# Two seams of a three-stage kernel re-ordered: one pair's weight sums on VectorE, other banks and an earlier first gate tile at the first seam

## The chip, the cores and the metric

The kernel runs on one core of a Trainium2 chip. The metric is the device time of one execution in microseconds (us), as the median of several runs; less is better. The engines are named as in the profile: PE is TensorE, DVE is VectorE, ACT is ScalarE, POOL is GpSimd, SP is SyncE, which issues most DMAs (its DMA queue is SPq).

## The reference

Attention with a decay by blocks, then two MLPs one after the other, all in float32:

```python
# q, k, v: (2, 8, 768, 64); lam: (8,)
for b in range(nb):                                  # blocks of 64 tokens
    intra = einsum('bhic,bhjc->bhij', qb, kb) * Dmask[None]
    intra = einsum('bhij,bhjd->bhid', intra, vb)
    inter = einsum('bhid,bhde->bhie', qb * lam_pow[None], kv_state)
    out[:, :, sl] = intra + inter
    kv_state = lam_block * kv_state + einsum('bhsd,bhse->bhde', kb_dec, vb)
x = out.transpose(0, 2, 1, 3).reshape(1536, 512)
h = x @ w_in                                         # 512 x 2048
x = (h * np.cos(h)) @ w_out                          # 2048 x 512
h = x @ w2_in
y = (h * (1.0 / (1.0 + np.exp(-h)))) @ w2_out        # 1536 x 512
```

## The kernel before

**Precision.** Every float32 operand of the MLPs is split in a high part (an ACT CAST, line 121) and a low part (value minus high part, line 122, on POOL unless an engine is named). A product is then three matmuls: high by high, low by high, high by low.

**Stages.** Attention runs over six chunks of 128 tokens per sequence. Then come four GEMMs: in 0 (to about 190 us of the trace), out 0 (to about 335), in 1 (to about 455), out 1. The stretch where attention and GEMM in 0 overlap (about 50 to 92 us) is called the passage. The first seam is the step from GEMM in 0 to out 0, the second from out 0 to in 1, the third from in 1 to out 1.

**GEMM in.** The 2048 hidden features are taken in eight pairs j of 256. For two thirds of the tokens (quad A) pair j is computed by seven products of sums of blocks in place of eight, A*j*.1 to A*j*.7 (`product(Q, i)`, 6 matmuls each, line 429). For the last third (quad B) it is plain: B*j*, 24 matmuls, line 445. Products 5, 6 and 7 need sums or differences of the weights of a pair:

- `rebias_w` (ACT, L106) and `convert_w` (DVE, L115 writes `sb`, L116 writes `w`) turn a loaded weight piece (`raw`) into floats.
- `sum_w` makes the four sums `S` of a pair (four 128x256 operations, L134).
- `split_plain` and `split_sums` make the split weights `win` from `w` and from `S`.

`copy_u`, `c22`, `c21` and `copy_ab` put the quad's results together. Each of the two halves of a quad, and each B, then passes the gate: `act_n` (ACT, L482), `act_s` (DVE, L491), `act_sin` (ACT, L498), `act_g` (DVE, L504), whose result goes to DRAM (`gd<-s`).

**GEMM out.** Features are taken in 16 pieces f of 128, tokens in thirds b = 0, 1, 2. `gemm_out(L, b, f, ms)` does four output blocks m, three matmuls each (line 703); b = 2 comes last, alone. In the text (b, f, lo) is m = 0, 1 and (b, f, hi) is m = 2, 3. The gate's results are loaded back (`gf`, by `load_half`, `load_halves`, `load_g`) and split into `gh` and `gl` (`prepare_half` for one third of one piece, `prepare` for two). Output weights pass `rebias_w`, `convert_w` and `split_out` (`wout`).

**PSUM.** There are three pairs of banks (`cab` 0, 1, 2, by `two_banks`) and two single ones (`d`, by `one_bank`). In GEMM in 0, A*j* uses pair j modulo 2 and every B uses pair 2. In GEMM out 0, third 0 uses pairs 0 and 1; third 1 uses pair 2 and the two single banks.

**Order.** `manual_schedule` means that each engine and queue executes its instructions in the order in which the code issues them. So the order of the calls in the body, and the dictionary `tasks`, which hangs weight work onto places of the loops, decide what stands behind what. Loads of weights go through one list (`load_next`). Tiles live in pools of few slots (`t4` four, `t2` five, `w` four): an instruction that writes a tile waits for the last reader of the slot's tile before.

Of the kernel before, what the change touches and what calls it, by code (L numbers as in the profile page):

```python
# [18 lines left out]
TB = 512  # L19
# [21 lines left out]
def tile_decay_attention__two_mlps(  # L41
# [12 lines left out]
    nc = tc.nc  # L54
# [5 lines left out]
    FT = DFF // P  # L60
# [82 lines left out]
        a = 0 if L == 0 else HB  # L143
        split(hi[:, TB + a:2 * TB], lo[:, TB + a:2 * TB], w1[:, a:])

    def split_sums(L, j):
        t = win[L, j]
        s = sums.pop((L, j))
        for i in range(2):
            u = slice(4 + 2 * i, 6 + 2 * i)  # L150
            split(t[:, 0, u], t[:, 1, u], s[:, 2 * i:2 * i + 2])

    def split_out(L, f):
        t = wring[f // 8].tile([P, 2, TB], F32R, name="wout")
# [3 lines left out]
    def pair_tasks(L, j, engine=nc.gpsimd):  # L158
        f = 2 * j
        return [  # L160
            lambda: rebias_w(L, f, 0),
            lambda: (rebias_w(L, f + 1, 0), convert_w(L, f, 0), load_next()),
            lambda: (convert_w(L, f + 1, 0), load_next()),
            lambda: sum_w(L, j, engine),
            lambda: split_plain(L, j),
            lambda: split_sums(L, j),
        ]

    def out_tasks(L, f):
# [246 lines left out]
    def product(Q, i):  # L416

        wu, xu, bank, start = PRODUCTS[i]
        if i == 1:
            n = Q.j if Q.L == 0 else quads.index(Q)  # L420
            Q.cab = two_banks(n % 2 if Q.L == 0 else (n + 2) % 3)
            Q.d = one_bank(n % 2)
            Q.banks = {"a": Q.cab[:, 0, 0:Q.n], "b": Q.cab[:, 1, 0:Q.n], "d": Q.d[:, 0:Q.n]}
            if Q.L == 0 and n < 2:
                nc.tensor.matmul(Q.cab[:, 1, :], zeros[:, 0:P], zeros, start=True, stop=True)
        w, (xh, xl) = win[Q.L, Q.j], xt[Q.L, Q.part]
        for m, (part, x) in enumerate(((0, xh), (1, xh), (0, xl))):
            for kt in range(2):
                nc.tensor.matmul(  # L429
                    Q.banks[bank],  # L430
                    w[:, part, wu, kt * P:(kt + 1) * P],
                    x[:, xu, kt, :],
                    start=start and m == 0 and kt == 0,
                    stop=m == 2 and kt == 1,
                    skip_group_check=True,
                )

    def plain(Q, i):

        if i == 0:  # L440
            Q.cab = two_banks(2)
        w, (xh, xl) = win[Q.L, Q.j], xt[Q.L, Q.part]
        for m, (part, x) in enumerate(((0, xh), (1, xh), (0, xl))):
            for kt in range(KT):
                nc.tensor.matmul(  # L445
                    Q.cab[:, i],
                    w[:, part, 2 * i + kt // 2, kt % 2 * P:(kt % 2 + 1) * P],
                    x[:, kt, :],
                    start=m == 0 and kt == 0,
                    stop=m == 2 and kt == KT - 1,  # L450
                )
# [58 lines left out]
    def gemm_in_0(tasks):  # L510
# [51 lines left out]
        act_g(old, 1)  # L562
        act_n(Bq, 0)
        act_s(Bq, 0)
        load_halves(0)
        load_g(0, 0, 2)
        load_g(0, 0, 3)
        gemm_out(0, 0, 0, (0, 1))
        task(FP, 1)
        act_sin(Bq, 0)  # L570
        act_g(Bq, 0)
        gemm_out(0, 0, 1, (0, 1))
        prepare_half(0, 1, 0)
        prepare_half(0, 1, 1)
        prepare(0, 0, 2)

    def gemm_in_1(tasks):
# [65 lines left out]
            for i in range(2):  # L643
                gf[L, 2, f + i] = t[:, i]

    def load_half(L, f):
        t = tpool.tile([P, TB], F32, tag="t2", name="gf", bufs=5)
        nc.sync.dma_start(out=t, in_=gd[L][f, :, 0:TB])
        gf[L, "half", 0, f] = t

    def load_halves(L):
        t = tpool.tile([P, 2, TB], F32, tag="t4", name="gf", bufs=4)
# [28 lines left out]
    def y_tiles(L, b):  # L681
        if (L, b) not in ys:
            if b == 1:
                t = two_banks(2)
                ys[L, b] = [t, None, t[:, 0], t[:, 1]] + [one_bank(i) for i in range(2)]
            else:
                t = [two_banks(i) for i in range(2)]
                ys[L, b] = t + [t[m // 2][:, m % 2] for m in range(4)]
        return ys[L, b]

# [90 lines left out]

    def gemm_outs(L, tasks):

        items = [x for f in range(FT + 2) for x in ((0, f), (1, f - 2)) if 0 <= x[1] < FT]
        items += [(2, f) for f in range(FT)]
        for b, f in items:
            if L == 1 and b == 2 and f >= FT - 2:
                break
            if b == 0:
                load_g(L, 0, f + 4)  # L790
                prepare(L, 0, f + 2)
# [9 lines left out]
            gemm_out(L, b, f, (2, 3) if b == 0 and f < 2 else range(4))  # L801
            for x in tasks.get((b, f), []):
                x()
        if L == 1:
# [5 lines left out]
    with tc.manual_schedule():  # L810
# [84 lines left out]
        A, c = quads_a, SC - 1  # L895
        att_scores(c, 0, ps_s, "s")
        split_sums(0, 0)
        product(A[0], 1)
        copy_ab(A[0])
        att_l(c - 1)  # L900
        att_scores(c, 1, ps_s, "s")
        rebias_w(0, 3, 0)
        convert_w(0, 3, 0)
        load_next()
        sum_w(0, 1, nc.gpsimd)
        product(A[0], 2)
# [26 lines left out]
        rebias_w(0, 4, 0)  # L933
        rebias_w(0, 5, 0)

        def place(tasks, at_n, fns):
            for i, x in enumerate(fns):
# [5 lines left out]
        for L in range(2):  # L943
            tasks = {}
            if L == 0:
                for j in range(2, FP):
                    f = 2 * j
                    if j > 2:
                        put((j - 2, 2), *(lambda f=f + i: rebias_w(0, f, 0) for i in range(2)))
                    for i in range(2):  # L950
                        put((j - 1, 0), lambda f=f + i: convert_w(0, f, 0), load_next)
                    put((j - 1, 0), lambda j=j: sum_w(0, j, nc.gpsimd))
                    put((j - 1, 1), lambda j=j: split_plain(0, j))
                    put((j - 1, 2), lambda j=j: split_sums(0, j))
                for n, f in ((6, 0), (6, 1), (7, 2), (7, 3)):
                    put((n, 2), lambda f=f: rebias_w(0, f, 1))
                    put((n + 1, 0), lambda f=f: convert_w(0, f, 1), load_next)
                    put((n + 1, 1), lambda f=f: split_out(0, f))
                put((FP - 1, 0), lambda: load_half(0, 0), lambda: load_half(0, 1))
                gemm_in_0(tasks)  # L960
            else:
                for j in range(2, FP):
                    at_n = min(4 * j - 8, 18)
                    for n, x in zip((0, 1, 2, 2, 3, 4), pair_tasks(L, j)):
                        put(at_n + n, x)
                for f, n in enumerate((20, 22, 24, 25)):
# [55 lines left out]
```

## Time and profile before

| | |
|---|---|
| median of 3 runs | 595.28 us (594.83, 597.52, 595.28) |
| the profiled execution | 592.26 us, its span 590.5 us |
| TensorE clock granted, mean of the span | 0.990 |
| PE busy | 564.3 us, 96% of the span |
| POOL busy | 350.9 us, 59% |
| DVE busy | 347.8 us, 59% |
| ACT busy | 295.7 us, 50% |

Times in the trace count from the span's start. The profiled execution is 1.8 us longer than its span and 3.0 us shorter than the median. A clock of 1.00 is TensorE's full 2.4 GHz, 0.50 is its other level of 1.2 GHz.

### The profile page before, as it was taken

What the parts mean: (1) busy time and instruction counts of PE and PEld (TensorE: products, weight loads), DVE (VectorE), ACT (ScalarE), POOL (GpSimd) and SP (SyncE); (2) the same over time, 40 slices, a digit from 0 to 9 for tenths busy, and PEclk for the clock granted to TensorE, in tenths of its full rate; (3) what the DMA queues carried; (4) which work ended last, traced back from release to release, by engine and by line L of the source; (5) the groups of instructions that cost most, each with busy time, mean ns of one, the idle gap of its engine ahead of it and who ended that gap; (6) DMA issues with size and microseconds to landing.
All of it is one profiled execution on the core that took longest, in us unless ns stands there. A gap on an engine that the chain in (4) does not pass through costs nothing.

```text
span 590.5 us, 8374 instructions
## 1 busy us (share of the span) xinstructions
PE 564.3 (96%) x3168; PEld 464.3 (79%) x3168; DVE 347.8 (59%) x355; ACT 295.7 (50%) x440; POOL 350.9 (59%) x261
## 2 busy tenths in 40 slices
PE   7999799999997699999999999999799999999997
PEld 4888587777776488888888788888689888888885
DVE  6689257776677599900499246667666799302001
ACT  4566267777776655310571365666656665201220
POOL 2688635555553699940489338555754699911541
PEclk9999999999998889999999999999999999999999
DMA  9999145445445886740044026455466896205501
GB/s 177 210 233 240 37 141 178 158 153 178 160 166 195 282 329 238 246 144 0 1 143 144 1 72 236 162 182 190 157 241 226 299 319 198 71 1 196 182 15 72
DMA packets 79640, 97.02 MB, mean 164 GB/s; under 512 B 40688, under 2 KB 57072, under 8 KB 79600
## 3 DMA queue, kind: packets, MB, share of 16 engines
q1 hardware_dynamic: 77360, 95.96, 50.8%
q10 hardware_dynamic: 2240, 0.53, 0.5%
q8 instruction: 25, 0.41, 0.3%
q14 instruction: 15, 0.12, 0.1%
HBM read 68.16 MB, written 28.31 MB: 163 GB/s over the span
## 4 chain that ended last, share of the span: by engine, by line
PE 72%; DVE 9%; POOL 6%; issue 4%; DMA 3%; ACT 3%; SPq 1%; ACTq 0%; DVEq 0%; POOLq 0%
PE cab L703 30%; PE cab L429 20%; PE d L429 8%; PE d L703 7%; PE cab L445 6%; DVE xal L122 2%; DVE S L134 2%; POOL win L122 2%; DVE sb L115 1%; DMA q<-in_q_dram 1%; DVE w L116 1%; ACT s L486 1%; DMA v<-in_v_dram 1%; POOL S L134 1%; DMA gf<-gd 1%
## 5 line engine op out<-in xcount | busy, mean ns | idle before, releaser
L122 POOL TENSOR_TENSOR gl<-gf,gh 128x512 fp32r<-128x512 f32 (+1 forms) x68 | 128.6, 1898 | 97.0 <-ACT gh L121 73.3
L703 PE MATMUL cab<-gh,wout 128*128 128x512 f32 x320 | 100.3, 395 | 2.4 <-ACT gh L121 2.4
L703 PE MATMUL cab<-wout,gh 128*128 128x512 f32 x320 | 98.6, 390 | 0.0
L121 ACT CAST gh<-gf 128x512 fp32r<-128x512 f32 (+1 forms) x68 | 53.5, 795 | 85.9 <-DMA out_dram<-o 29.3
L116 DVE SCALAR_TENSOR_TENSOR w<-w,sb 128x512 uint32<-128x512 uint32 x64 | 90.1, 1408 | 9.5 <-ACT w L106 3.2
L429 PE MATMUL cab<-xah,win 128*128 128x512 f32 x320 | 86.9, 394 | 0.2 <-ACT cab L459 0.2
L703 PEld LDWEIGHTS cab<-gh,wout 128*128 128x128 f32 x320 | 61.2, 191 | 15.6 <-ACT gh L121 2.8
L134 POOL TENSOR_TENSOR S<-w 128x256 f32<-128x256 f32 x28 | 30.6, 1091 | 69.6 <-DVE w L116 69.6
L703 PEld LDWEIGHTS cab<-wout,gh 128*128 128x128 f32 x320 | 59.9, 188 | 12.1
L429 PEld LDWEIGHTS cab<-xah,win 128*128 128x128 f32 x320 | 58.9, 188 | 12.8 <-ACT cab L459 0.6
L703 PE MATMUL cab<-gl,wout 128*128 128x512 f32 x160 | 63.7, 398 | 3.9 <-POOL gl L122 3.9
L122 POOL TENSOR_TENSOR wout<-w,wout 128x512 fp32r<-128x512 f32 x32 | 51.4, 1612 | 21.1 <-ACT wout L121 21.1
L115 DVE TENSOR_SCALAR sb<-raw 128x512 uint32<-128x512 uint32 x64 | 61.0, 954 | 3.0 <-DMA raw<-in_moe_w_out_dram 2.0
L703 PE MATMUL cab<-wout,gl 128*128 128x512 f32 x160 | 62.3, 389 | 0.0
L122 POOL TENSOR_TENSOR win<-S,win 128x512 fp32r<-128x512 f32 x32 | 46.5, 1474 | 7.6 <-ACT win L121 7.6
L429 PE MATMUL cab<-xal,win 128*128 128x512 f32 x160 | 49.5, 391 | 0.0
L466 ACT COPY u<-cab 128x512 f32<-128x512 f32 (+1 forms) x48 | 24.6, 513 | 46.9 <-PE cab L429 46.9
L778 DVE COPY o<-cab 128x512 f32<-128x512 f32 x10 | 6.7, 689 | 67.7 <-PE cab L703 65.3
L106 ACT ACTIVATE w<-raw 128x512 f32<-128x512 f32 x64 | 41.9, 671 | 7.3 <-POOL wout L122 3.4
L429 PE MATMUL d<-xah,win 128*128 128x512 f32 x128 | 36.9, 400 | 5.7 <-POOL win L122 2.7
L703 PEld LDWEIGHTS cab<-gl,wout 128*128 128x128 f32 x160 | 30.6, 191 | 11.5 <-POOL gl L122 5.3
L504 DVE TENSOR_TENSOR s<-cab,s 128x1024 f32<-128x1024 f32 (+1 forms) x32 | 34.7, 1084 | 7.0 <-ACT s L486 5.5
(125 smaller groups left out, 976.4 us busy)
## 6 DMA issues: line engine op xcount, KB each, us to landing
gf<-gd SPq DMA_DIRECT2D x46, 512.0 KB, 4.6
gd<-s SPq DMA_DIRECT2D x40, 512.0 KB, 3.1
raw<-in_moe_w_in_dram SPq DMA_DIRECT2D x32, 512.0 KB, 4.3
raw<-in_moe_w_out_dram SPq DMA_DIRECT2D x32, 512.0 KB, 4.6
gd<-s SPq DMA_DIRECT2D x16, 256.0 KB, 2.1
v<-in_v_dram SPq DMA_DIRECT2D x12, 256.0 KB, 6.3
out_dram<-o SPq DMA_DIRECT2D x12, 256.0 KB, 2.1
k<-in_k_dram SPq DMA_DIRECT2D x6, 256.0 KB, 5.7
```

The source lines that it names most:

```text
L106: nc.scalar.activation(w, raw[piece][:, :, 1].bitcast(F32), AF.Prelu, scale=2.0**-112, alpha=-(2.0**32))
L115: nc.vector.tensor_scalar(out=sb, in0=r[:, :, 0], scalar1=2.0**-29, scalar2=7.0, op0=ALU.mult, op1=ALU.min)
L116: nc.vector.scalar_tensor_tensor(out=w, in0=w, scalar=3, in1=sb, op0=ALU.logical_shift_left, op1=ALU.bitwise_or)
L121: nc.scalar.copy(hi, of)
L122: (engine or nc.gpsimd).tensor_tensor(out=lo, in0=of, in1=hi.bitcast(F32), op=ALU.subtract)
L134: engine.tensor_tensor(out=s[:, i], in0=x, in1=y, op=op)
L429: nc.tensor.matmul(Q.banks[bank], w[:, part, wu, kt * P:(kt + 1) * P], x[:, xu, kt, :], start=start and m == 0 and kt == 0, stop=m == 2 an ...
L445: nc.tensor.matmul(Q.cab[:, i], w[:, part, 2 * i + kt // 2, kt % 2 * P:(kt % 2 + 1) * P], x[:, kt, :], start=m == 0 and kt == 0, stop=m == ...
L466: nc.scalar.copy(t, Q.banks["b"])
L504: nc.vector.tensor_tensor(out=t, in0=source(Q, i), in1=t, op=ALU.mult)
L703: nc.tensor.matmul(y[m], x, z, start=f == 0 and n == 0, stop=f == FT - 1 and n == 2)
L778: nc.vector.tensor_copy(o, ys[1, b][2 + m])
```

## The change

Five edits, none of which changes what is computed.

1. Passage. Pair 1's `sum_w` and the low parts of its `split_sums` are issued on DVE in place of POOL, and that `split_sums` comes ahead of product A0.6 (it came behind `c22` of A0). `rebias_w` of piece 3 is issued a product earlier. Pair 2's conversion, two weight loads and `sum_w` (on POOL) come ahead of A1.7; its two splits are hung one place earlier in the loop.
2. `split_sums` takes an engine, and the two pairs of MLP 1 that are prepared in GEMM out 0 give it DVE, as their `sum_w` had already.
3. First seam. The last B uses pair 0. GEMM out 0 uses pair 2 and then 1 for third 0, and pair 0 for third 1. The two loads of 512 KB and the halves' loads are replaced by four `load_half` at pair 7's first place; the two `prepare_half` of third 1 are issued earlier.
4. `gemm_outs`: the first pieces are taken in another order, third 1 follows one piece behind third 0 and no longer two, `copy_a` and the sends are hung accordingly.
5. GEMM in 1: pair 7's weight tasks and those of the first four output pieces are hung one or two places later. The order of the bank pairs is renamed to fit 3.

```diff
-    def split_sums(L, j):
+    def split_sums(L, j, engine=None):
...
-            split(t[:, 0, u], t[:, 1, u], s[:, 2 * i:2 * i + 2])
+            split(t[:, 0, u], t[:, 1, u], s[:, 2 * i:2 * i + 2], engine)
...
-            lambda: split_sums(L, j),
+            lambda: split_sums(L, j, engine),
...
-            Q.cab = two_banks(n % 2 if Q.L == 0 else (n + 2) % 3)
+            Q.cab = two_banks(n % 2 if Q.L == 0 else (0, 2, 1)[n % 3])
...
-            Q.cab = two_banks(2)
+            Q.cab = two_banks(2 if Q.j < FP - 1 else 0)
...
-        load_halves(0)
         load_g(0, 0, 2)
         load_g(0, 0, 3)
         gemm_out(0, 0, 0, (0, 1))
-        task(FP, 1)
+        prepare_half(0, 1, 0)
         act_sin(Bq, 0)
         act_g(Bq, 0)
         gemm_out(0, 0, 1, (0, 1))
-        prepare_half(0, 1, 0)
         prepare_half(0, 1, 1)
+        task(FP, 1)
         prepare(0, 0, 2)
...
-                t = two_banks(2)
+                t = two_banks(0)
...
-                t = [two_banks(i) for i in range(2)]
+                t = [two_banks(i) for i in (2, 1)]
...
-        items = [x for f in range(FT + 2) for x in ((0, f), (1, f - 2)) if 0 <= x[1] < FT]
-        items += [(2, f) for f in range(FT)]
+        lo, hi = (0, 1), (2, 3)
+        items = [(1, 0, hi), (1, 1, hi), (0, 0, hi), (0, 1, hi)]
+        items = (items if L == 0 else items[2:] + items[:2]) + [(1, 0, lo), (1, 1, lo)]
+        items += [(*x, range(4)) for f in range(2, FT + 1) for x in ((0, f), (1, f - 1)) if 2 <= x[1] < FT]
+        items += [(2, f, range(4)) for f in range(FT)]
...
+        rebias_w(0, 3, 0)
         product(A[0], 1)
...
-        rebias_w(0, 3, 0)
         convert_w(0, 3, 0)
         load_next()
-        sum_w(0, 1, nc.gpsimd)
+        sum_w(0, 1, nc.vector)
...
+        split_sums(0, 1, nc.vector)
         product(A[0], 6)
...
-        split_sums(0, 1)
+        for i in range(2):
+            rebias_w(0, 4 + i, 0)
+            convert_w(0, 4 + i, 0)
+            load_next()
+        sum_w(0, 2, nc.gpsimd)
         product(A[1], 7)
...
-                put((FP - 1, 0), lambda: load_half(0, 0), lambda: load_half(0, 1))
+                put((FP - 1, 0), *(lambda i=i, f=f: load_half(0, i, f) for i in range(2) for f in range(2)))
...
-                    at_n = min(4 * j - 8, 18)
+                    at_n = min(4 * j - 8, 19)
...
-                for f, n in enumerate((20, 22, 24, 25)):
-                    place(tasks, n - 1, out_tasks(L, f))
+                for f, n in enumerate((21, 23, 24, 26)):
+                    place(tasks, n, out_tasks(L, f))
```

DVE at the passage, from the conversion of piece 3 (`convert_w`) to attention's last output `xbl`; lines with + are new:

```order
 L115 TENSOR_SCALAR sb<-raw 128x512
 L116 SCALAR_TENSOR_TENSOR w<-w,sb 128x512
+L134 TENSOR_TENSOR S<-w 128x256
+L134 TENSOR_TENSOR S<-S,w 128x256
+L134 TENSOR_TENSOR S<-w 128x256
+L134 TENSOR_TENSOR S<-w,S 128x256
+L122 TENSOR_TENSOR win<-S,win 128x512 x2
 L390 TENSOR_TENSOR xbl<-pso,xbh 128x2x4x128
```

Six instructions now stand between the conversion and `xbl`. Pair 2's conversion also moves on DVE, to behind `c22` of A0.

ACT at the first seam, from the sine of A7's second half to the first whole gate tile (`gh` 128x1024); before:

```order
137 L498 ACTIVATE s<-s,consts 128x1024
138 L482 ACTIVATE s<-cab,consts 128x1024
139 L121 CAST wout<-w 128x512 x2
140 L498 ACTIVATE s<-s,consts 128x1024
141 L121 CAST gh<-gf 128x512 x2
142 L121 CAST gh<-gf 128x1024
```

Now, where row 140 is again the sine of B7:

```order
139 L121 CAST gh<-gf 128x512
140 L498 ACTIVATE s<-s,consts 128x1024
141 L121 CAST gh<-gf 128x512
142 L121 CAST wout<-w 128x512 x2
143 L121 CAST gh<-gf 128x1024
144 L106 ACTIVATE w<-raw 128x512 x3
```

The first `gh` of third 1 stands ahead of B7's sine, the second right behind it, and the output weights 2 and 3 behind both.

PE at the first seam, from B7's last matmuls. Before, `cab_1928` and `cab_1929` are third 0's two pairs of banks, `wout_1815` and `wout_1818` are pieces 0 and 1, `wout_1936` is piece 2 (rows of the same kind left out):

```order
301 L445 MATMUL cab_1869<-xbl_844,win_1693 128x512 x4
302 L703 MATMUL cab_1928<-gh_1884,wout_1815 128x512 x2
...
309 L703 MATMUL cab_1928<-gl_1885,wout_1818 128x512
310 L703 MATMUL cab_1929<-gh_1884,wout_1815 128x512 x2
...
317 L703 MATMUL cab_1929<-gl_1885,wout_1818 128x512
318 L703 MATMUL cab_1928<-gh_1884,wout_1936 128x512 x2
```

Now `cab_1930` and `cab_1931` are third 0's pairs, `cab_1959`, `d_1960` and `d_1961` third 1's, `wout_1819` and `wout_1822` pieces 0 and 1, `wout_1951` piece 2:

```order
302 L702 MATMUL cab_1930<-gh_1888,wout_1819 128x512 x2
...
310 L702 MATMUL d_1960<-gh_1888,wout_1819 128x512 x2
...
314 L702 MATMUL d_1960<-gh_1888,wout_1822 128x512 x2
...
318 L702 MATMUL cab_1931<-gh_1888,wout_1819 128x512 x2
...
326 L702 MATMUL cab_1959<-gh_1888,wout_1819 128x512 x2
...
334 L702 MATMUL cab_1930<-gh_1888,wout_1951 128x512 x2
```

Third 1's pieces 0 and 1 now stand ahead of piece 2, their hi blocks (rows 310 to 317) ahead of third 0's. Piece 2 is reached after 48 matmuls of the GEMM in place of 24.

## Rows read from the trace of the kernel before

**Rows 1.** Timeline of PE at the passage: start, length, instruction, idle before and its releaser.

```profile
70.08 0.73 PE L429 MATMUL d<-xah,win 128*128 128x512 f32 x2 [1.71 <-ACT win L121]
72.13 0.73 PE L429 MATMUL d<-xah,win 128*128 128x512 f32 x2 [1.32 <-POOL win L122]
...
91.78 0.73 PE L429 MATMUL d<-xah,win 128*128 128x512 f32 x2 [1.42 <-POOL win L122]
```

**Rows 2.** Timelines of DVE and POOL at the passage.

```profile
60.50 0.69 DVE L116 SCALAR_TENSOR_TENSOR w<-w,sb 128x512 uint32<-128x512 uint32 x1
...
69.58 2.49 POOL L122 TENSOR_TENSOR win<-S,win 128x512 fp32r<-128x512 f32 x2 [2.83 <-ACT win L121]
82.93 1.59 POOL L134 TENSOR_TENSOR S<-w 128x256 f32<-128x256 f32 x1 [10.86 <-DVE w L116]
```

**Rows 3.** Timeline of DVE at the second seam: two sums and a low part.

```profile
300.08 2.33 DVE L122 TENSOR_TENSOR xal<-T,xah 128x1024 fp32r<-128x1024 f32 x1
302.33 0.41 DVE L134 TENSOR_TENSOR S<-w 128x256 f32<-128x256 f32 x1
...
304.09 1.52 DVE L134 TENSOR_TENSOR S<-w 128x256 f32<-128x256 f32 x1
```

**Rows 4.** The chain that ended last, in order of time, at the first seam.

```profile
181.75 1.39 PE d L429 x6
...
205.06 6.16 PE cab L703 x16
...
212.57 4.08 PE cab L703 x18
```

**Rows 5.** Timeline of PE at the first seam.

```profile
186.26 3.52 PE L445 MATMUL cab<-xbh,win 128*128 128x512 f32 x8 [3.14 <-DVE s L504]
...
201.39 0.73 PE L703 MATMUL cab<-gh,wout 128*128 128x512 f32 x2 [2.40 <-ACT gh L121]
205.06 0.79 PE L703 MATMUL cab<-gl,wout 128*128 128x512 f32 x1 [2.94 <-POOL gl L122]
```

**Rows 6.** Windows of PE: us, PE busy, granted clock, DMA share, GB/s.

```profile
72.00:73.00 1.00, 0.87 (x4) 1.00 0.00 0
186.00:187.00 1.00, 0.74 (x2) 0.50 0.00 0
203.00:204.00 1.00, 0.00 (x0) 0.51 0.62 162
```

**Rows 7.** Timelines of SP, ACT, DVE, POOL at the first seam; the page's DMA issues.

```profile
186.14 0.37 SPq L506 DMA_DIRECT2D gd<-s  x1
...
186.50 0.60 ACT L121 CAST gh<-gf 128x512 fp32r<-128x512 f32 x1
188.01 1.15 ACT L498 ACTIVATE s<-s,consts 128x1024 f32<-128x1024 f32 x1 [0.91 <-DVE s L491]
...
191.41 1.22 DVE L504 TENSOR_TENSOR s<-h,s 128x1024 f32<-128x1024 f32 x1
...
187.18 1.95 POOL L122 TENSOR_TENSOR gl<-gf,gh 128x512 fp32r<-128x512 f32 x1 [0.28 <-ACT gh L121]
...
gd<-s SPq DMA_DIRECT2D x40, 512.0 KB, 3.1
```

**Rows 8.** Timelines of DVE at the start of GEMM out 0, from 205 us.

```profile
205.39 2.68 DVE L116 SCALAR_TENSOR_TENSOR w<-w,sb 128x512 uint32<-128x512 uint32 x1
208.11 2.49 DVE L115 TENSOR_SCALAR sb<-raw 128x512 uint32<-128x512 uint32 x1
```

**Rows 9.** Timelines of POOL and PE at the second seam.

```profile
324.48 2.73 POOL L122 TENSOR_TENSOR win<-S,win 128x512 fp32r<-128x512 f32 x2
...
328.49 0.50 PE L703 MATMUL cab<-gl,wout 128*128 128x512 f32 x1 [0.92 <-POOL gl L122]
```

**Rows 10.** Timelines of ACT and PE in GEMM in 1.

```profile
416.08 0.67 ACT L106 ACTIVATE w<-raw 128x512 f32<-128x512 f32 x1 [2.12 <-POOL win L122]
...
418.08 0.74 PE L429 MATMUL cab<-xbh,win 128*128 128x256 f32 x4 [1.88 <-ACT cab L459]
```

More of the change, by code (lines that the diff above doesn't have):

```diff
@@ L644, in load_g, with load_half @@
                 gf[L, 2, f + i] = t[:, i]
-    def load_half(L, f):
+    def load_half(L, i, f):
         t = tpool.tile([P, TB], F32, tag="t2", name="gf", bufs=5)
-        nc.sync.dma_start(out=t, in_=gd[L][f, :, 0:TB])
-        gf[L, "half", 0, f] = t
+        nc.sync.dma_start(out=t, in_=gd[L][f, :, i * TB:(i + 1) * TB])
+        gf[L, "half", i, f] = t
     def load_halves(L):
@@ L782, in gemm_outs @@
     def gemm_outs(L, tasks):
-        items = [x for f in range(FT + 2) for x in ((0, f), (1, f - 2)) if 0 <= x[1] < FT]
-        items += [(2, f) for f in range(FT)]
-        for b, f in items:
+        lo, hi = (0, 1), (2, 3)
[3 more added lines that the diff above has]
+        items += [(2, f, range(4)) for f in range(FT)]
+        for b, f, ms in items:
             if L == 1 and b == 2 and f >= FT - 2:
                 break
+            if f < 2 and b < 2:
+                gemm_out(L, b, f, ms)
+                if b == 0:
+                    load_g(L, 0, f + 4)
+                elif ms == lo:
+                    prepare(L, 0, f + 2)
+                for x in tasks.get((b, f), []) if ms == hi else []:
+                    x()
+                continue
             if b == 0:
@@ L800, in gemm_outs @@
                 prepare(L, 2, f + 2)
-            gemm_out(L, b, f, (2, 3) if b == 0 and f < 2 else range(4))
+            gemm_out(L, b, f, ms)
             for x in tasks.get((b, f), []):
@@ L932, in tile_decay_attention__two_mlps @@
         act_s(A[0], 0)
-        rebias_w(0, 4, 0)
-        rebias_w(0, 5, 0)
         def place(tasks, at_n, fns):
@@ L949, in tile_decay_attention__two_mlps @@
                         put((j - 2, 2), *(lambda f=f + i: rebias_w(0, f, 0) for i in range(2)))
[L950 to L954, printed above, removed]
+                        for i in range(2):
+                            put((j - 1, 0), lambda f=f + i: convert_w(0, f, 0), load_next)
+                        put((j - 1, 0), lambda j=j: sum_w(0, j, nc.gpsimd))
+                    early = j == 2
+                    put((j - 1, 1 - early), lambda j=j: split_plain(0, j))
+                    put((j - 1, 2 - early), lambda j=j: split_sums(0, j))
                 for n, f in ((6, 0), (6, 1), (7, 2), (7, 3)):
@@ L962, in tile_decay_attention__two_mlps @@
                 for j in range(2, FP):
-                    at_n = min(4 * j - 8, 18)
+                    at_n = min(4 * j - 8, 19)
                     for n, x in zip((0, 1, 2, 2, 3, 4), pair_tasks(L, j)):
                         put(at_n + n, x)
-                for f, n in enumerate((20, 22, 24, 25)):
-                    place(tasks, n - 1, out_tasks(L, f))
-                put(24, *(lambda f=f: load_half(1, f) for f in range(2)))
+                for f, n in enumerate((21, 23, 24, 26)):
+                    place(tasks, n, out_tasks(L, f))
+                put(24, *(lambda f=f: load_half(1, 0, f) for f in range(2)))
                 put(28, lambda: load_halves(1), lambda: prepare_half(1, 0, 0))
@@ L979, in tile_decay_attention__two_mlps @@
                 for u in range(2):
-                    tasks.setdefault((1, FT - 3 + u), []).append(lambda u=u: copy_a(u))
+                    put((1, FT - 2), lambda u=u: copy_a(u))
                 tasks.setdefault((1, FT - 1), []).append(lambda: kept.setdefault("a", keep_a()).pop(0)())
@@ L988, in tile_decay_attention__two_mlps @@
                 for m in range(4):
-                    tasks.setdefault((1, FT - 3 + m // 2), []).append(lambda m=m: send(0, m))
+                    put((1, FT - 2 + m // 2), lambda m=m: send(0, m))
                     tasks.setdefault((2, m), []).append(lambda m=m: send(1, m))
```

## The prediction

> **What bounds the kernel now.** The table puts TensorE (PE) at 96% of the span, so a change of order can only win back what PE loses: its waits, and stretches at the low clock. I read PE's timeline for its waits, the other engines' timelines for what each wait was for, the chain for sums over many matmuls, and windows for the clock. Four places lie in the reach of the diff.
>
> At the passage PE waits three times for weight sums: 1.71 and 1.32 us in A1.7, 1.42 in A2.7 [rows 1]. At the first seam it waits 3.14, 2.40 and 2.94 us [rows 5], and its clock falls to half around these waits [rows 6]. At the second seam it waits 0.92 us [rows 9], in GEMM in 1 1.88 us [rows 10].
>
> **The base of the sum.** The durations are those of the execution of 592.26 us, 3.0 us under the median of 595.28. I take the gain from the trace and subtract it from the median.
>
> **Passage: sums on DVE.** Before, A1.7 is due at 70.08 - 1.71 = 68.37 [rows 1], but pair 1's low parts start on POOL at 69.58 and take 2.49 us [rows 2]. Now DVE goes on after the conversion, which ends at 60.50 + 0.69 = 61.19 [rows 2]. A sum on DVE took 0.41 us, and 1.52 with POOL at work beside it [rows 3]: four take 1.6 to 6.1 us, done at 62.9 to 67.3. The ACT cast of a half takes 0.6 [rows 7]. The low part of 128x512 is bounded by the two-input operation of that size, 0.69 [rows 2], and by half of 2.33, 1.2 [rows 3]. So both are done by 62.9 + 0.6 + 1.4 = 64.9 at best and 67.3 + 0.6 + 2.4 = 70.3 at worst. POOL works beside it for only part of this time, on pair 1's plain split, so I take about 67, ahead of 68.37: the whole 1.71 + 1.32 = 3.03 goes. The worst end leaves 1.9 of it.
>
> The Trainium skill speaks against this move: its page "SBUF — State Buffer", section "Who interferes with whom", says that a DVE instruction with two SBUF inputs contends with a GpSimd instruction that reads SBUF. The spread from 0.41 to 1.52 agrees with it; if it held for every instruction here, the worst end would count, and the passage would win 2.5 in place of 4.4.
>
> What stands behind the six added DVE instructions is attention's `xbl`, and `c22`. Even from 70.3 they are two operations of about 1.2 and 0.7 us. PE needs `xbl` only for the first plain B, behind A1.7, A0.3 and A0.4, whose 18 matmuls take 4.1 us [rows 4], and `c22`'s bank not before. So I cost the delay at nothing; without that cover it is what the worst end is over 68.37, 2 us.
>
> Pair 2: the conversion stood behind the gate's operations on DVE, so POOL idled 10.86 us and started its sums at 82.93 [rows 2]. Now the conversion comes right behind `c22`. That waits for A0.5, which ends where A1.7 is due, at 68.4, and for a copy of 0.6; with 0.7 for itself and four operations of 0.4 to 0.7 [rows 2, 3] POOL starts at about 72, at worst at 74.4 (from 70.3). Its chain before lasted from 82.93 to the 91.78 at which PE went on [rows 1, 2]: 8.9 us. So it now ends at 81 to 83, against A2.7 at 91.78 - 1.42 - 3.03 = 87.3. The 1.42 goes, with 4 us in hand. Sum of the passage: 3.03 + 1.42 = 4.45, say **4.4**; range 2.5 to 4.5.
>
> **First seam: what it loses now.** A7.4 ends at 181.75 + 1.39 = 183.14, and the long stretch that runs without a wait begins at 212.57 [rows 4]. Between them PE does B7's 24 matmuls and 48 of GEMM out. At full speed 18 take 4.08 us [rows 4], so 72 take 16.3. The stretch lasts 29.4: **13.1 us are lost**, 3.14 + 2.40 + 2.94 = 8.5 in waits [rows 5] and 4.6 at the low clock: 16 matmuls took 6.16 in place of 3.6 [rows 4].
>
> **What it loses then.** B7 takes pair 0, free since A6, so the 3.14 goes: B7 runs 183.1 to 188.6, and (0,0,lo) and (0,1,lo) with their 12 matmuls to 191.3. Next on PE is third 1's hi part, whose `gh` must come by way of ACT:
> - B7's first gate step needs a tile's slot, freed when B6's store lands: issued at 186.14, 3.1 us [rows 7], so 189.2; the sine before it on ACT ends at 188.01 + 1.15 = 189.2 as well [rows 7]. The step takes some 1.1: 190.3.
> - The first `gh` of third 1, 0.6 [rows 7]: 190.9. Its `gl` on POOL, 1.95 at most [rows 7], 1.25 at least (half of 2.49, [rows 2]): 192.1 to 192.9. (1,0,hi) thus ends at 193.1 to 193.8, 0.5 to 1.1 late.
> - The second `gh` stands behind B7's sine (the ACT rows above), the sine behind `act_s` on DVE, and that behind `act_g` of A7, 191.41 + 1.22 = 192.6 [rows 7]. With 1.2 for `act_s`, 1.15 for the sine, 0.6 for the cast: 195.6. Then `gl`, to 196.9 to 197.5.
>
> So the change **makes a new wait**: PE idles 1.8 to 2.5 us for the second `gh`, about 0.9 to 1.5 more for its `gl`. (1,1,hi) ends near 198.2 where without waits it would end at 194.0. That is 3.8 to 4.5 lost, 5.9 if `act_g` is slowed by POOL as the sums above. The 36 matmuls of pieces 0 and 1 that then precede piece 2 need nothing new except B7's banks, which `act_g` of B7 has read by about 197, before (1,0,lo) at 201. Piece 2's `gl` is due at 203.7. Its load is issued where 512 KB stood in the queue before; I estimate 202 to 204, so up to 0.6 more: 4.8 lost as my value. Gain 13.1 - 4.8 = **8.3**; range 13.1 - 8.0 = 5.1 (with the low clock, below) to 9.3.
>
> **Second seam.** The 0.92 wait is for a `gl` that POOL could start only when pair 1's low parts were through (324.48, 2.73 us [rows 9]). These go to DVE, so POOL starts `gl` 2.7 us sooner. DVE, busy without a pause there, gets four more operations of 0.7 to 1.2 [rows 2, 3]: 3 to 5 us in all, in front of the first copies of the output, which may cost PE up to 0.5. Gain **0.7**, range -0.5 to 0.9.
>
> **GEMM in 1.** ACT's rebias of the first output piece waits 2.12 us for a slot that POOL frees late, and the copy that PE needs stands behind it: 1.88 [rows 10]. The rebias now comes two places later, when the slot is free: the wait goes. But pair 7's sums now come a place later as well, and their margin before is not known from a wait; a new one there can be bounded by that which goes and half a microsecond, 2.4. Gain **1.5**, range -0.5 to 1.9.
>
> The third seam shows no wait of PE before; the other order there is costed at nothing, since PE's own matmuls cover the loads; without them it is a wait like one of the first seam's, up to 3 us [rows 5].
>
> **Sum:** 4.4 + 8.3 + 0.7 + 1.5 = 14.9; 595.28 - 14.9 = 580.4. The low ends give 2.5 + 5.1 - 0.5 - 0.5 = 6.6, so 588.7; the high ends 4.5 + 9.3 + 0.9 + 1.9 = 16.6, so 578.7.
>
> **Rivals.**
>
> *The clock falls in the new wait.* At the passage 1.71 and 1.32 us of waiting left the clock at 1.00; at the seam it was at half after the waits of 3.14 and of 2.40 and 2.94 [rows 1, 5, 6]. The new one, 1.8 to 2.5 and then 0.9 to 1.5 with two matmuls between, lies between these. Price: 16 matmuls cost 2.5 more at half speed, so 1.5 to 2.5, and about 582.5. The Trainium skill's page "TensorE: Matmul & The Clock Gate", section "HAM oscillation — how this bites in real kernels", describes waits that throttle the clock again in each turn of a loop; by it this wait would cost twice. Which side it falls on no row here shows.
>
> *The new orders only half work.* POOL's low parts and DVE's gate step slow each other at the seam as 0.41 and 1.52 show [rows 3], the second `gh` comes 2 us later and the clock falls: the seam wins 5, the passage 2.5 and the rest 1: 8.5 in all, 586.8. For it: the seam's chain passes ACT, DVE, ACT, POOL in turn, with no slack at any step. Against: at 191.41 DVE took its plain 1.22 [rows 7].
>
> *Nothing is gained: the waits only move.* A wait removed comes back at the next due thing, such as B7's `gh` at the seam, and PE's sum is the same: 595. Against: at the seam 13.1 us were lost, and no step of the new chain is 13 long.
>
> *Slower: GEMM out is paced by DVE.* With third 1 one piece behind, PE wants a new piece of weights each 24 matmuls, 24 x 4.08/18 = 5.44 us [rows 4]. DVE's conversion of a piece took 2.49 + 2.68 = 5.17 at its slowest [rows 8], 0.27 under this. If it rose over 5.44, PE would wait in each of the 12 pieces from 4 on. To eat the gain of 14.9 it would need 14.9 / 12 = 1.2 more, 6.7 us per piece; from 6.9 the kernel is slower by 3 us, about 598. The rows stay 1.5 under that.
>
> **How the numbers follow.** The forecast with its own scatter (578 to 582) has 0.45, the clock's fall 0.25, the half working orders 0.20, moved waits 0.06, slower 0.04. The predicted time is the likeliest, a little up towards its neighbour: 580.8. The range from 577.5 (the high ends, and a microsecond for the scatter of the median, whose runs lie 2.7 apart) to 588 leaves out the last two, the worst of the half working cases and a little at the fast end. A measurement of this kernel can tell about 0.5%, 3 us. Faster by more than that: 0.45 + 0.25 + 0.20 + a little of the moved waits, 0.91; within it 0.05; slower 0.04.
>
> **What would show it.** After the change PE's timeline has no wait near 68 to 70 and 87 to 90, and DVE's four sums stand right behind the conversion, each under 1.5 us. At the seam B7 starts without a gap behind A7.4, and the only long waits are for `gh` and `gl` of third 1's second piece, 3 to 4 us together; from A7.4's end to the end of the 72 matmuls it takes about 21 us in place of 29.4. The windows there show whether the clock stayed at 1.00. The waits of 0.92 and 1.88 are gone. I am wrong if PE shows waits of a microsecond in each piece of GEMM out, if pair 2's sums still end after A2.7 is due, or if a wait I don't name, in the third seam for one, exceeds 3 us.

## The result and the profile after

The changed kernel takes 579.25 us (median of 4 runs, 577.94 to 580.2) beside 595.06 of the kernel before in the same comparison: a ratio of 0.973, 95% interval 0.9689 to 0.9772. That is 15.8 us, where 14.9 were forecast. In a second comparison the ratio was 0.9729 (0.97 to 0.9758). The profiled execution took 577.94 us, its span 576.2; that of before 590.5, so the trace shows 14.3 us of the gain. By stretches of the two traces these are 4.7 up to the end of A7.4, 6.0 in the first seam (to piece 2), 0.2 in the rest of GEMM out 0, 3.6 in GEMM in 1, and -0.2 in GEMM out 1.

The engines' line of the page, and the view of PE's waits (what PE waited for: us in total, times, longest):

```profile
PE 562.6 (98%) x3168; PEld 463.8 (81%) x3168; DVE 355.3 (62%) x365; ACT 294.0 (51%) x440; POOL 338.4 (59%) x251
```

```profile
PE d L702 <- ACT gh L121: 3.9, 1, 3.9
...
PE cab L702 <- POOL gl L122: 0.8, 1, 0.8
```

From the passage's start on PE has only these two waits of over half a microsecond. None of those at the passage [rows 1] or in GEMM in 1 [rows 10] is there. The first of the two is new, as forecast, and longer than forecast.

**Passage.** DVE's timeline, then POOL's and PE's:

```profile
60.59 1.57 DVE L116 SCALAR_TENSOR_TENSOR w<-w,sb 128x512 uint32<-128x512 uint32 x1
62.26 1.33 DVE L134 TENSOR_TENSOR S<-w 128x256 f32<-128x256 f32 x1
63.62 1.38 DVE L134 TENSOR_TENSOR S<-S,w 128x256 f32<-128x256 f32 x1
64.93 0.41 DVE L134 TENSOR_TENSOR S<-w 128x256 f32<-128x256 f32 x1
65.26 0.41 DVE L134 TENSOR_TENSOR S<-w,S 128x256 f32<-128x256 f32 x1
65.69 1.36 DVE L122 TENSOR_TENSOR win<-S,win 128x512 fp32r<-128x512 f32 x2
```

```profile
73.33 0.73 POOL L134 TENSOR_TENSOR S<-w 128x256 f32<-128x256 f32 x1 [8.61 <-DVE w L116]
...
80.20 3.56 POOL L122 TENSOR_TENSOR win<-S,win 128x512 fp32r<-128x512 f32 x2
```

```profile
69.35 1.07 PE L429 MATMUL d<-xah,win 128*128 128x512 f32 x4
```

The four sums stand behind the conversion, two at 1.3 to 1.4 us and two at 0.41, between the bounds 0.41 and 1.52 [rows 3]. Pair 1 is complete at 67.05, 2.3 us ahead of A1.7 at 69.35, which has no wait. Pair 2 starts on POOL at 73.3 in place of 82.93 [rows 2] and is through at 83.8.

**First seam.** PE, from the end of A7.4 over B7's start to piece 2:

```profile
178.00 0.61 PE L429 MATMUL d<-xal,win 128*128 128x512 f32 x2
178.45 2.04 PE L445 MATMUL cab<-xbh,win 128*128 128x512 f32 x8
...
192.53 1.22 PE L702 MATMUL d<-gh,wout 128*128 128x512 f32 x2 [3.85 <-ACT gh L121]
...
201.91 0.62 PE L702 MATMUL cab<-gh,wout 128*128 128x512 f32 x2
```

B7 follows A7.4 without a gap: the 3.14 us for its banks [rows 5] are gone. The 72 matmuls run from 178.45 to 201.91, 23.5 us in place of 29.4 [rows 4], where 21 were forecast. PE idles 3.85 us for the second `gh` of third 1. The windows of PE (us, busy, granted clock, DMA share, GB/s) show the clock go down in this wait and stay down behind it:

```profile
189.00:190.00 1.00, 0.00 (x0) 1.00 0.83 201
190.00:191.00 1.00, 0.00 (x0) 0.66 0.83 328
...
196.00:197.00 1.00, 1.00 (x3) 0.50 1.03 389
197.00:198.00 1.00, 1.00 (x5) 0.93 0.99 404
```

Why the `gh` is late stands in the timelines of DVE, POOL and ACT:

```profile
184.10 1.34 DVE L115 TENSOR_SCALAR sb<-raw 128x512 uint32<-128x512 uint32 x1
...
186.27 1.45 DVE L115 TENSOR_SCALAR sb<-raw 128x512 uint32<-128x512 uint32 x1
...
188.43 1.22 DVE L504 TENSOR_TENSOR s<-h,s 128x1024 f32<-128x1024 f32 x1
189.57 1.22 DVE L491 SCALAR_TENSOR_TENSOR s<-cab,s 128x1024 f32<-128x1024 f32 x1
```

```profile
181.95 3.21 POOL L122 TENSOR_TENSOR gl<-gf,gh 128x512 fp32r<-128x512 f32 x2 [7.12 <-ACT gh L121]
```

```profile
185.46 0.61 ACT L121 CAST gh<-gf 128x512 fp32r<-128x512 f32 x1
190.82 1.15 ACT L498 ACTIVATE s<-s,consts 128x1024 f32<-128x1024 f32 x1 [4.75 <-DVE s L491]
191.88 0.60 ACT L121 CAST gh<-gf 128x512 fp32r<-128x512 f32 x1
```

The first `gh` (185.46) is early. Then ACT stands 4.75 us in front of B7's sine, whose input DVE writes only at 189.57 to 190.8: behind A7's last gate step (188.43), and that behind the conversion of output weights 2 and 3, from 184.10. In the trace of before the first instruction of that conversion was shorter:

```profile
189.04 0.41 DVE L115 TENSOR_SCALAR sb<-raw 128x512 uint32<-128x512 uint32 x1
```

**Second seam.** PE and POOL:

```profile
314.85 0.50 PE L702 MATMUL cab<-gl,wout 128*128 128x512 f32 x1 [0.81 <-POOL gl L122]
```

```profile
310.48 2.64 POOL L122 TENSOR_TENSOR win<-w,win 128x512 fp32r<-128x512 f32 x2
313.08 4.21 POOL L122 TENSOR_TENSOR gl<-gf,gh 128x512 fp32r<-128x512 f32 x3
```

The wait of 0.92 [rows 9] has become one of 0.81, one piece earlier: the `gl` now stands behind the plain split of the pair in place of that of its sums.

**GEMM in 1** runs from 322.69 to 440.06, 117.4 us; before it ran from 333.60 to 454.53, 120.9. Its first matmul and the first of out 1 in PE's timeline:

```profile
322.69 1.07 PE L429 MATMUL cab<-xah,win 128*128 128x512 f32 x4
...
440.06 0.63 PE L702 MATMUL cab<-wout,gh 128*128 128x512 f32 x2
```

### The profile page after: what moved, and what is told of

Read it like the earlier page. It is cut to its first block, busy times and chain, and to the rows that moved or that the text cites. A ratio compares the mean times of both kernels' runs of the same rounds, so it can differ in the third digit from the quotient of the medians.

```text
span 576.2 us, 8373 instructions
## 1 busy us (share of the span) xinstructions
PE 562.6 (98%) x3168; PEld 463.8 (81%) x3168; DVE 355.3 (62%) x365; ACT 294.0 (51%) x440; POOL 338.4 (59%) x251
## 4 chain that ended last, share of the span: by engine, by line
PE 85%; POOL 4%; DMA 4%; issue 3%; ACT 1%; DVE 1%; SPq 1%; POOLq 0%; ACTq 0%; DVEq 0%
PE cab L702 36%; PE cab L429 23%; PE d L429 9%; PE d L702 7%; PE cab L445 7%; DMA v<-in_v_dram 2%; POOL gl L122 1%; POOL xal L395 1%; DMA gf<-gd 1%; PE psc L328 1%; DMA lamb<-in_lam_dram 1%; PE pso L350 1%; SPq L241 1%; POOL kd L291 1%; POOL sdec L318 1%
## 5 line engine op out<-in xcount | busy, mean ns | idle before, releaser
L122 POOL TENSOR_TENSOR gl<-gf,gh 128x512 fp32r<-128x512 f32 (+1 forms) x68 | 133.6, 1970 | 94.9 <-ACT gh L121 71.0
L702 PE MATMUL cab<-gh,wout 128*128 128x512 f32 x320 | 99.1, 391 | 0.0
L115 DVE TENSOR_SCALAR sb<-raw 128x512 uint32<-128x512 uint32 x64 | 81.0, 1265 | 3.5 <-DMA raw<-in_moe_w_out_dram 2.5
L116 DVE SCALAR_TENSOR_TENSOR w<-w,sb 128x512 uint32<-128x512 uint32 x64 | 71.1, 1112 | 9.2 <-ACT w L106 3.0
L134 POOL TENSOR_TENSOR S<-w 128x256 f32<-128x256 f32 x26 | 27.3, 1048 | 71.3 <-DVE w L116 71.3
L122 POOL TENSOR_TENSOR wout<-w,wout 128x512 fp32r<-128x512 f32 x32 | 47.3, 1484 | 19.5 <-ACT wout L121 19.5
L121 ACT CAST wout<-w 128x512 fp32r<-128x512 f32 x32 | 19.7, 620 | 41.7 <-DVE w L116 41.7
L122 POOL TENSOR_TENSOR win<-w,win 128x512 fp32r<-128x512 f32 (+1 forms) x32 | 39.5, 1258 | 2.2 <-ACT win L121 2.2
L122 POOL TENSOR_TENSOR win<-S,win 128x512 fp32r<-128x512 f32 x26 | 36.7, 1434 | 3.7 <-ACT win L121 3.7
```

What stands on the lines that cost most here:

```text
L115: nc.vector.tensor_scalar(out=sb, in0=r[:, :, 0], scalar1=2.0**-29, scalar2=7.0, op0=ALU.mult, op1=ALU.min)
L116: nc.vector.scalar_tensor_tensor(out=w, in0=w, scalar=3, in1=sb, op0=ALU.logical_shift_left, op1=ALU.bitwise_or)
L121: nc.scalar.copy(hi, of)
L122: (engine or nc.gpsimd).tensor_tensor(out=lo, in0=of, in1=hi.bitcast(F32), op=ALU.subtract)
L134: engine.tensor_tensor(out=s[:, i], in0=x, in1=y, op=op)
L702: nc.tensor.matmul(y[m], x, z, start=f == 0 and n == 0, stop=f == FT - 1 and n == 2)
```

## The experiments

All kernels are the changed one with the edit shown. A thousandth in a ratio is 0.6 us; the changed kernel has 0.973, and each ratio is to the kernel before, timed on the same chip. Clear of the changed kernel's interval (0.9689 to 0.9772) are only the passage undone and the last two kernels of the seam. The intervals of all the others overlap with it, so there the traces carry more of the reading than the times.

### The passage undone

```diff
-        rebias_w(0, 3, 0)
         product(A[0], 1)
...
+        rebias_w(0, 3, 0)
...
-        sum_w(0, 1, nc.vector)
+        sum_w(0, 1, nc.gpsimd)
...
-        split_sums(0, 1, nc.vector)
...
-        sum_w(0, 2, nc.gpsimd)
+        split_sums(0, 1)
```

Pair 2's conversion, sums and splits, too, are back at their old places in the loop.

> Edit 1 alone is undone (sums of pair 1 on POOL, split behind c22, pair 2 prepared in the loop). If the passage won what its three waits cost, they come back: 1.71, 1.32 and 1.42, and with about 0.2 more for each as the trace before shows (A1.7 took 4.80 us where it takes 1.37 without waits, 3.03 of it idle), 5 us in all: about 584.3 beside 579.25. If the waits there only were slack for what follows, the time moves by under 2 us.

Measured: 585.43 us, ratio 0.9825 (0.9801 to 0.985), 5.7 us more than the changed kernel. PE's timeline and a window:

```profile
70.95 0.73 PE L429 MATMUL d<-xah,win 128*128 128x512 f32 x2 [1.71 <-ACT win L121]
73.00 1.22 PE L429 MATMUL d<-xah,win 128*128 128x512 f32 x2 [1.32 <-POOL win L122]
...
94.22 0.73 PE L429 MATMUL d<-xah,win 128*128 128x512 f32 x2 [1.43 <-POOL win L122]
```

```profile
74.00:76.00 2.00, 2.00 (x6) 0.50 0.00 0
```

The three waits are back to within a hundredth. In this execution the clock went to half behind the first two; in the trace of before the same two waits left it at 1.00 [rows 6].

### Only the engine undone

```diff
-        sum_w(0, 1, nc.vector)
+        sum_w(0, 1, nc.gpsimd)
...
-        split_sums(0, 1, nc.vector)
+        split_sums(0, 1)
```

> Of the passage's edit only the engine is undone: pair 1's sums and their low parts are on POOL again, in the new, earlier place. If VectorE is what made pair 1 ready in time, A1.7 waits again: POOL's sums end at about 65.5 in the changed kernel's trace time, its plain split at 68, its low parts at 70.6, against A1.7 due at 69.35: 1 to 1.5 us lost, pair 2 untouched. If the place alone did it, nothing moves. If VectorE's sums cost other work time, the kernel gets faster.

Measured: 577.59 us, ratio 0.9701 (0.9678 to 0.9724): no loss. POOL's timeline, ACT's and PE's:

```profile
66.99 2.54 POOL L122 TENSOR_TENSOR win<-S,win 128x512 fp32r<-128x512 f32 x2
```

```profile
58.41 0.68 ACT L106 ACTIVATE w<-raw 128x512 f32<-128x512 f32 x1 [1.98 <-DMA raw<-in_moe_w_in_dram]
```

```profile
59.62 1.20 PE L429 MATMUL cab<-xah,win 128*128 128x512 f32 x4 [1.54 <-ACT cab L459]
...
70.21 1.07 PE L429 MATMUL d<-xah,win 128*128 128x512 f32 x4
```

POOL, too, is through with pair 1 at 69.5, and A1.7 starts at 70.21 without a wait. In this execution PE had lost 1.54 us before, for another reason (below); without them A1.7 would be due at 68.7 and would, as I estimate from these rows, have waited some 0.4 us for its second half. So it is the new place of `split_sums`, and pair 2's, that win the passage; VectorE adds those 0.4 us at most, and the times show none of it.

The 1.54 is a wait that the change brings: the rebias of piece 3 now stands on ACT ahead of the copy in A0's banks, and when its weights land late, as here, the copy and PE wait with it. In the changed kernel's profiled execution they were there in time.

### Third 0's hi blocks first

```diff
-        items = (items if L == 0 else items[2:] + items[:2]) + [(1, 0, lo), (1, 1, lo)]
+        items = items[2:] + items[:2] + [(1, 0, lo), (1, 1, lo)]
```

> In GEMM out 0 third 0's hi blocks of pieces 0 and 1 come ahead of third 1's, as in GEMM out 1. If the 7.1 us that the first seam still loses are PE's wait for the second gh of third 1 (3.85, then 0.84 for its gl) and the low clock behind it, 12 matmuls of work (2.7 us) now lie in that wait: it shrinks to about 1.2 us, the clock stays at 1.00, and the 72 matmuls take about 19 us in place of 23.5. The gl of piece 2, done at 199.0 in the trace of the changed kernel, is then the next thing PE waits for (about 2 us), so the whole gains about 2.9 us: 576.3 beside 579.25. If the seam's length is set by something else, the time does not move.

Measured: 575.99 us, ratio 0.9688 (0.9658 to 0.9719), 2.5 us under the changed kernel. The wait is 1.99 us, not 1.2, and the clock still fell in the profiled execution:

```profile
194.16 1.14 PE L702 MATMUL d<-gh,wout 128*128 128x512 f32 x2 [1.99 <-ACT gh L121]
```

```profile
194.00:196.00 2.00, 1.62 (x3) 0.57 0.94 311
```

The size came out, the clock did not. The mean clocks of the four executions were 0.996, 0.999, 1.000 and 1.000. By these it falls in some and not in others; where, only the profiled one shows.

### The wait filled

```diff
+                if (L, b, f, ms) == (0, 1, 0, hi):
+                    for _ in range(16):
+                        nc.tensor.matmul(y_tiles(0, 0)[1][:, 0], zeros[:, 0:P], zeros, start=True, stop=True)
```

> 16 matmuls of zeros into a bank that is not yet in use stand on PE behind third 1's first hi blocks, 3.4 us of work that no result uses, in the place of the wait of 3.85 us. The wait's end does not move. If the clock fell because PE idled there, it now stays at 1.00 and the stretch from A7.4 to the end of the 72 matmuls shortens by what the low clock cost, 2.2 us, to about 21.2: about 577. If the clock fell for another reason, or its fall costs nothing, the time is that of the changed kernel, 579.25.

Measured: 576.53 us, ratio 0.9698 (0.9668 to 0.9728), 1.9 us under the changed kernel. The trace is plainer (PE's timeline, then a window):

```profile
188.57 3.63 PE L795 MATMUL cab<-zeros 128*128 128x512 bf16 x15
192.57 0.73 PE L702 MATMUL d<-gh,wout 128*128 128x512 f32 x2 [0.37 <-ACT gh L121]
...
200.41 0.61 PE L702 MATMUL cab<-gh,wout 128*128 128x512 f32 x2
```

```profile
194.00:196.00 2.00, 2.00 (x9) 1.00 1.01 399
```

One of the 16 records is missing from the trace. The `gh` comes no sooner (14.6 us behind the start of B7, 14.1 in the changed kernel), the clock stays at 1.00, and from there to piece 2 it takes 200.41 - 192.57 = 7.84 us in place of 201.91 - 192.53 = 9.38: the fall of the clock costs 1.5 us here. The whole stretch takes 22.5 us in place of 23.5, not the 21.2 expected, since the fall costs 1.5 us and not 2.2, and the `gh` itself comes half a microsecond later.

### The second gh ahead of the sine

```diff
         prepare_half(0, 1, 0)
+        prepare_half(0, 1, 1)
         act_sin(Bq, 0)
...
-        prepare_half(0, 1, 1)
         task(FP, 1)
```

> The second gh of third 1 is issued ahead of B7's sine on ACT. If the sine, and DVE's work ahead of it, is what held that gh, it is there at about 186 and its gl at 188.7, PE's wait of 3.85 goes, and the next wait is that for piece 2's gl at 199.0, some 3 us: the whole gains 2.9 us at best (576.3), and about 0.7 if the clock falls in that new wait. If another thing held it (the load of gf), nothing moves.

Measured: 575.18 us, ratio 0.9682 (0.9652 to 0.9713), 2.9 us under the changed kernel. PE's waits are now for B7's bank and for piece 2's `gl`, and the clock stayed at 1.00:

```profile
194.69 0.70 PE L702 MATMUL cab<-gh,wout 128*128 128x512 f32 x2 [1.42 <-DVE s L504]
...
199.70 0.50 PE L702 MATMUL cab<-gl,wout 128*128 128x512 f32 x1 [1.59 <-POOL gl L122]
```

### The conversion late

```diff
         act_g(old, 0)
-        task(FP, 0)
         plain(Bq, 1)
...
         act_s(Bq, 0)
+        task(FP, 0)
         load_g(0, 0, 2)
```

> DVE's conversion of output weights 2 and 3, and the loads behind it, are issued behind B7's first DVE gate step in place of ahead of A7's last one. If the four conversion instructions (184.10 to 188.5 in the changed kernel's trace) are what made the last act_g, the sine, the second gh and the store ahead of the loads of pieces 2 and 3 late, all of these come about 3.8 us sooner: gh at 188, piece 2's gl near 195, one wait of about 1 us is left and the clock stays: 5 to 6 us gained, about 573.7. If the conversion is itself urgent, the output weights of pieces 2 and 3 become the new wait, and the gain is under 2 us.

Measured: 575.19 us, ratio 0.9676 (0.9645 to 0.9706), 3.2 us under the changed kernel, not 5 to 6. The wait for `gh` went, as expected, to 0.42 us, with 1.13 for its `gl` behind it. The conversion, now where POOL is nearly idle, was short again:

```profile
188.51 0.44 DVE L115 TENSOR_SCALAR sb<-raw 128x512 uint32<-128x512 uint32 x1
```

Piece 2's `gl` did not come sooner, since ACT waited for its load, which is now issued right behind the two weight loads (ACT's and PE's timelines):

```profile
197.73 1.05 ACT L121 CAST gh<-gf 128x1024 fp32r<-128x1024 f32 x1 [6.06 <-DMA gf<-gd]
```

```profile
201.28 0.50 PE L702 MATMUL cab<-gl,wout 128*128 128x512 f32 x1 [1.71 <-POOL gl L122]
```

### Loads first, the conversion late, the gh ahead of the sine

```diff
         act_s(Bq, 0)
         load_g(0, 0, 2)
         load_g(0, 0, 3)
+        task(FP, 0)
```

This comes with the two edits above; the gate's loads now stand ahead of the weight loads.

> The conversion of output weights 2 and 3 late, the second gh ahead of B7's sine, and the loads of the gate's pieces 2 and 3 ahead of the two weight loads on the queue. In the run with the late conversion alone piece 2's load was issued at 190.7 behind two weight loads and landed 7.0 us later, its gl was ready at 201.2 and PE waited 1.71 us for it. If the queue's order is what holds piece 2, its load now goes out near 188.5, its gl is ready near 196, and the seam is left with about 1.5 us of waits: 5.5 us under the changed kernel, about 573.7, and 1.5 to 2 under the late conversion alone. If the load waits for its slot in any case, the time is that of the late conversion alone, 575.

Measured: 572.45 us, ratio 0.9636 (0.9612 to 0.966). The changed kernel was run beside it on the same chip:

> The changed kernel once more, on the chip of the two below. Its ratio to the kernel before should again be 0.973 within 0.003; the seam's wait of 3.85 us for gh recurs and the mean clock is about 0.994.

Measured: 577.74 us, ratio 0.9729 (0.97 to 0.9758), with a wait of 3.84 us and mean clocks of 0.994 and 0.997. So the kernel with the loads first is 5.5 us under it. One wait of size is left, for piece 3, and the mean clock was 1.000 in three of four executions:

```profile
200.40 0.50 PE L702 MATMUL cab<-gl,wout 128*128 128x512 f32 x1 [1.66 <-POOL gl L122]
```

One more was run, with the hi blocks first and pair 1's two splits at the second seam at place 12 in place of 10 and 11:

> The same with third 0's hi blocks first, and pair 1's two splits of MLP 1 two places later in GEMM out 0. If the wait of 0.8 us there is for a gl queued behind pair 1's plain split on POOL, it goes: 0.8 us under the kernel with the loads first, and the seam wins up to another 0.5: about 572.5. If GEMM in 1 then waits for pair 1's weights, it is lost again.

Measured: 572.41 us, ratio 0.963 (0.9609 to 0.9651): the same. Neither kernel shows the wait of 0.8 at the second seam, though the first doesn't touch it. The late conversion lacks it too, and so does the passage with only the engine undone, whose second `gh` at the seam comes at 193.45 and not at 192.53. So an earlier start is not what removes it; the cause stays open.

### GEMM in 1's places undone

```diff
-                    at_n = min(4 * j - 8, 19)
+                    at_n = min(4 * j - 8, 18)
...
-                for f, n in enumerate((21, 23, 24, 26)):
-                    place(tasks, n, out_tasks(L, f))
+                for f, n in enumerate((20, 22, 24, 25)):
+                    place(tasks, n - 1, out_tasks(L, f))
```

> Edit 5 alone is undone: pair 7's and the first output pieces' weight tasks stand at their old places in GEMM in 1. GEMM in 1 took 120.9 us before and 117.4 after. If the places are what won this, the waits of 1.88 and 1.21 us come back and the kernel takes about 3.5 us more, 582.8. If the order of bank pairs or the other edits won it, nothing moves.

Measured: 582.48 us, ratio 0.9777 (0.975 to 0.9804), 2.8 us more. GEMM in 1 takes 121.0 us again (323.90 to 444.86), and both waits are back:

```profile
408.39 0.73 PE L429 MATMUL cab<-xbh,win 128*128 128x256 f32 x4 [1.88 <-ACT cab L459]
...
416.14 1.19 PE L429 MATMUL d<-xah,win 128*128 128x512 f32 x4 [1.23 <-DVE h L474]
```

### The second seam's engine undone

```diff
-            lambda: split_sums(L, j, engine),
+            lambda: split_sums(L, j),
```

> Edit 2 alone is undone: in GEMM out 0 the low parts of two pairs' sums are on POOL again. The prediction gave this edit 0.7 us; in the changed kernel's trace a wait of 0.81 for a gl is still there, behind another split on POOL. If the wait has only changed its cause, undoing the edit changes the time by under 0.5 us. If the prediction's size holds, 0.7 us are lost; if POOL is now later by the 7 us of these four operations, more than 2.

Measured: 577.81 us, ratio 0.9708 (0.9684 to 0.9732): no loss. In the trace the wait is the old one again, 0.92 behind the sums' split of 2.73 us (POOL's and PE's timelines):

```profile
313.32 2.73 POOL L122 TENSOR_TENSOR win<-S,win 128x512 fp32r<-128x512 f32 x2
```

```profile
317.33 0.50 PE L702 MATMUL cab<-gl,wout 128*128 128x512 f32 x1 [0.92 <-POOL gl L122]
```

## Why the prediction was right, and where it was not

The sum came out (14.9 forecast, 15.8 measured), and so did its order: the first seam and the passage carry most of it. Two of its four terms were too large (by 2.3 and 0.7) and two too small (by 1.3 and by 1.3 to 2.1), so that the sum came out to 0.9 is in part luck. So is that the time lies at the forecast though the clock fell: the prediction had given that case 582.5 and the smaller chance.

**Passage, 4.4 forecast, 5.7 measured.** The waits went as the working said. Pair 1 was ready 4.9 us behind the conversion's end, where it said 5.8; that both come to about 67 is chance, since the conversion ended 1.0 later. The 5.7 is what undoing the edit costs; the traces of before and after, in which the clock held here, differ by 4.7 up to the end of A7.4. What the working left out is that a wait costs more than its idle time: the lost clock in some executions, and some 0.2 us around each wait. The step "sums on DVE" named the wrong half of the edit: with the sums on POOL in the new place nothing is lost. The Trainium skill's page "SBUF — State Buffer", section "Who interferes with whom", cited against the move, agrees with sums of 1.33 and 1.38 us while POOL split pair 1's weights and 0.41 after. It decided nothing here, as either engine was in time to within 0.4 us.

**First seam, 8.3 forecast, 6.0 found** (29.4 less 23.5, from the traces; no run undoes this edit). B7's bank came free as worked out, and the new wait is the one that was named, for the second `gh` behind B7's sine. The step that failed is the row on which its due time rested: A7's last `act_g` was taken from where it stood before, at 191.41 [rows 7]. In the new kernel everything ahead starts 4.7 us sooner, so it should have stood at 186.7; it stood at 188.43. The conversion ahead of it took two instructions of 1.34 and 1.45 us where the trace before had 0.4 each, since POOL's `gl` work (181.95 to 185.2 and 186.15 to 187.4) now lay beside it; in the run with the late conversion, where POOL was nearly idle, they took 0.44 and 0.43. So the wait was 3.85 and not 1.8 to 2.5. Then the first rival came true: the clock fell behind that wait. Its price was given as 1.5 to 2.5; the filled wait shows 1.5. The two together are more than the 2.3 us that the term was too large: the wait for the second `gl`, for which 0.9 to 1.5 were allowed, and the 0.6 for piece 2's `gl` do not show among PE's waits.

The prediction's 582.5 for that rival was too slow nevertheless, because the passage's and GEMM in 1's terms were too small. The Trainium skill's page "TensorE: Matmul & The Clock Gate", section "HAM oscillation — how this bites in real kernels", describes a loop in which each wait for a DMA throttles the clock again. The rows agree for the wait of 3.85 us. The waits of that loop are longer than the 1.8 to 2.5 us forecast here, so that this one "would cost twice" did not follow from the page alone; the last part shows shorter waits with either outcome.

**Second seam, 0.7 forecast, 0 found.** The step "POOL starts `gl` 2.7 us sooner" holds for that `gl`. What it missed is that POOL's other split, the plain one of 2.64 us, stands ahead of the `gl` of the piece before, and takes the same time. Undoing the edit changes nothing. In some of the later kernels the wait is not there at all, and why is open, so what the edit is worth in those is not known.

**GEMM in 1, 1.5 forecast, 2.8 to 3.6 found** (by the ratio of the undone kernel, and by the length of GEMM in 1 in the traces). The 1.88 went as worked out. The step that failed is the bound of 2.4 us on a new wait for pair 7: there is none. And the second wait of 1.2 us, for `c21`, went too; I had not counted it. It stands in PE's timeline of before:

```profile
425.83 1.18 PE L429 MATMUL d<-xah,win 128*128 128x512 f32 x4 [1.21 <-DVE h L474]
```

In the trace of before four conversion instructions stood ahead of `c21` on DVE; that they were the cause is read from the order there and was not tried by itself.

**The other rivals.** That waits only move, and that DVE paces GEMM out, did not come: GEMM out runs from piece 2 to its end without a wait for DVE. The half-working orders came in part. The second `gh` was 1.7 us late, where that rival had 2, and the clock fell; but POOL slowed the conversion and not the gate step, the seam still won 6.0 in place of 5, and the passage and GEMM in 1 lost nothing.

## What to carry to other kernels

When a change moves a stretch of work, take the due times of the new order and let the durations move with the neighbours: an instruction that ran alone before may run beside another engine's work afterwards. Before an operation is handed to another engine, try it in the new place on the old engine; the place alone may be what was wanted. And after a wait has been removed at a seam, look at the order in each queue that the next one hangs on: here three short moves, of a cast, a conversion and two loads, were worth 5.5 us more.

## What was not expected of the hardware

The same waits do not always have the same effect on TensorE's clock. In the trace of before, waits of 1.71 and 1.32 us left it at 1.00; with the passage undone, the same waits, to the hundredth, were followed by 0.50 for some three microseconds (73 to past 76 us). Eleven executions of the kernel before on the chip of that run had mean clocks between 0.982 and 0.991. A profiled execution that lies at the fast end of its runs, as that of before did (592.26 beside a median of 595), so shows a little less loss than the median has, which is in line with the 14.3 us of the traces beside 15.8 of the medians.

Matmuls of zeros in the place of the wait kept the clock at 1.00: nothing but the filling differed, and the `gh` came no sooner. A single wait of 1.99 us, with third 0's hi blocks first, was followed by a mean clock of 0.57 over two microseconds, so PE need not idle for as long as 3.85 us.

On DVE the conversion's first instruction, which reads one tensor only, took 0.41 to 0.44 us alone and 1.34 to 1.45 beside POOL's `gl`. So it is not only operations with two inputs that lose time there.
